# Memory rows turned in two column parts, two first products that trade banks, and later transfers in segment 0

## The chip, the cores and the metric

The kernel runs on one core of a Trainium2 chip. A core has TensorE (PE, matrix products; its weight loads are shown apart as PEld), VectorE (DVE), ScalarE (ACT), GpSimd (POOL) and SyncE (SP, which here only issues DMAs). Each works through its own instructions in order; semaphores hold an instruction until others have finished. SBUF is the working memory of 128 partitions, PSUM the memory that matrix products write to, in eight banks of 512 fp32 columns. The metric is device microseconds of one execution; the time of a kernel is the median of its runs.

## The reference, cut to what matters

The program is two blocks on x of 2048 rows by 640. The first is attention that runs through the rows in 64 segments of 32 rows, with 8 memory rows that each segment hands to the next:

```python
for s in range(n_seg):                      # 64, one after the other
    xs = x[:, s*seg_len:(s+1)*seg_len, :]   # 32 rows, normalised before
    h = concatenate([mem, xs], axis=1)      # 40 rows
    q, k, v = h @ Wq, h @ Wk, h @ Wv        # 32 heads of 128, from 640
    scores = where(mask, q @ k.T * scale, -1e9)
    o = softmax(scores) @ v @ Wo            # 40 rows of 640
    mem = o[:, :8]                          # the next segment's memory
    outs.append(o[:, 8:])
h  = x + concatenate(outs)
h2 = h + (relu(layernorm(h) @ w1 + b1) ** 2) @ w2 + b2
```

The memory makes the segments a chain: no query, key or value of a segment can be finished before the output rows of the memory of the segment before it.

## The kernel before, in words

The order of the instructions on every engine is the order of the program (a manual schedule), written out by hand; buffers come from pools, and a buffer is free again when the last reader in that order has been passed.

One segment is one call of `step`. Its 32 "main" columns are the 8 memory rows and the first 24 rows of the segment; they lie transposed in hT (640 in five chunks of 128, chunk c at column c x 160). The last 8 rows of each segment (the "tails") do not depend on the memory in their projections, so four segments' tails are projected together, as spare units of four matmuls that a planner (`plan`, `portion`) spreads over the segments at about eight a segment. The lists fill, late, mid and nook hold spare units, turns of evacuated tails, and statistics and normalisations of coming blocks; `run` and `run_late` take from them at fixed places.

On TensorE a segment runs: first query product (16 of the 32 heads, 20 matmuls, four to each chunk), first key product, second query product, second key product, memory scores (sm), value products, token scores, some spare units, values (po), the output product of the memory columns (pw, 64 matmuls, line 268), spare units, the token values of the segment before, spare units. Then the next segment's first query product needs the memory.

The way from pw to it: `wo_out` has ScalarE copy two halves of the partitions of pw crosswise into tmp (lines 281 and 282, name otmp), VectorE adds them to the blocks of pw on its own partitions (line 283) and gives o, 128 partitions by 160 columns, five groups of 32. `mem_to_hT` has VectorE turn o in 32 x 32 squares into hT (line 374): group f of o gives the memory columns of chunk f.

PSUM: the pool mm has three banks that rotate (`mmtile`), chn has one (tag ch, used in turn by pw, the first query product pq, and sm twice), pop has four (po; `potile` borrows them for px). In the last segment `end_output` puts the output product of an earlier segment, in chn, between the second query product and the first key product, which in this segment comes only there.

SP issues nearly all DMAs, in order. At the start it loads Wv, Wq, Wk and Wo. Tail values go to a DRAM buffer vt_d, row by row (line 337), and come back in another order as vt (line 394). Some rows wait in buffers that are needed later ("parked"); their stores stand in the list writes. Before the first segments the loop runs up to four of these stores, and in segment 0 loads x of block 1 and the tail values of segments 1 to 3. Then segment 0 runs its spare units (`SEG0`, in four portions among its output product), whose rows are stored when they are ready; their four row buffers are the ones that segment 1's query and key rows take next.

## Time and profile before

| | us |
|---|---|
| median of 3 runs (lowest to highest) | 974.47 (972.43 to 975.36) |
| the profiled execution, its own time | 971.71 |
| its span | 969.6 |
| PE busy | 937.7 (97%) |
| PEld busy | 546.9 (56%) |
| DVE busy | 652.6 (67%) |
| ACT busy | 524.5 (54%) |
| POOL busy | 280.5 (29%) |

The granted TensorE clock is 0.998 of full speed over the span. A line of the timeline gives start, duration, engine, line of the kernel, operation, what it writes and reads, the shape, and how many such instructions are merged; in brackets is idle time of the engine before it and what ended it. "PE pq L232" is a product into the tile pq; L232 is the helper `proj`, so all projections have this line. A matmul's end is modelled, and its duration overlaps the next, so lengths of work on PE are read from starts. In the list of waits each row has microseconds in total, number of times, and the longest.

### The profile page before, as it was taken

The page shows a single profiled execution, that of the slowest core. Times are in us where ns is not written, and L with a number is a line of the kernel's source. Part 1 is how long each engine was busy: PE and PEld are TensorE (multiplying, and loading weights), DVE is VectorE, ACT ScalarE, POOL GpSimd, SP SyncE. Part 2 cuts the span into 40 slices and gives each one's busy share as a digit, 9 for nine tenths or more (in the row PEclk, how much of TensorE's full clock was granted, in tenths as well). Part 3 has the DMA queues.
Part 4 walks back from the last instruction along what each step waited for, and adds up shares of the span by engine and source line. Part 5 has one row for each costly group of instructions (what it writes and reads, how often), then busy time and mean ns, then how long its engine had stood idle before and what let it go on. Part 6 is the DMA issues. An engine that isn't in the chain of part 4 may idle for free.

```text
span 969.6 us, 55554 instructions
## 1 busy us (share of the span) xinstructions
PE 937.7 (97%) x24749; PEld 546.9 (56%) x24760; DVE 652.6 (67%) x1942; ACT 524.5 (54%) x1271; POOL 280.5 (29%) x870
## 2 busy tenths in 40 slices
PE   6978999999999999999999999999999999999998
PEld 2445555555555555555555656555555656555555
DVE  5256777677777767777767676777776777566542
ACT  2445656565566655656656565656555655523321
POOL 2122323233223232322232323232323233253300
PEclk9999999999999999999999999999999999999999
DMA  9981100010010101010102010101010211543320
GB/s 357 399 275 45 23 17 20 19 27 21 19 27 18 30 14 31 9 32 7 37 9 32 13 31 12 33 12 33 12 33 6 53 40 23 182 125 80 98 55 28
DMA packets 65871, 56.62 MB, mean 58 GB/s; under 512 B 37384, under 2 KB 61712, under 8 KB 63712
## 3 DMA queue, kind: packets, MB, share of 16 engines
q1 hardware_dynamic: 65392, 52.74, 19.0%
q8 instruction: 194, 3.18, 1.4%
q14 instruction: 45, 0.37, 0.1%
q0 software_dynamic: 224, 0.33, 0.1%
q10 hardware_dynamic: 16, 0.01, 0.0%
HBM read 38.37 MB, written 9.44 MB: 49 GB/s over the span
## 4 chain that ended last, share of the span: by engine, by line
PE 85%; DVE 5%; DMA 4%; SPq 2%; ACT 2%; issue 1%; POOL 0%; ACTq 0%; DVEq 0%; POOLq 0%
PE ps L232 27%; PE pw L268 15%; PE px L232 13%; PE pq L232 7%; PE y L1012 6%; PE ps L960 6%; PE ps L268 3%; PE po L522 2%; DMA wq<-in_A_Wq_dram 2%; PE po L415 2%; SPq L149 2%; PE sm L486 1%; PE ps L575 1%; DMA wo<-in_A_Wo_dram 1%; DVE kT L476 1%
## 5 line engine op out<-in xcount | busy, mean ns | idle before, releaser
L232 PEld LDWEIGHTS <-hT 128*32 128x32 bf16 x7680 | 192.2, 96 | 191.5 <-DVE hT L374 23.4
L268 PE MATMUL pw<-wo,oT 128*32 128x320 bf16 x4224 | 160.9, 300 | 3.5 <-issue 1.8
L232 PE MATMUL ps<-wk,hT 128*32 128x512 bf16 x2520 | 158.0, 379 | 0.0
L268 PEld LDWEIGHTS <-oT 128*32 128x32 bf16 x4224 | 120.3, 97 | 40.6 <-DVE oT L242 19.4
L256 DVE STREAM_TRANSPOSE qT<-row 128x512 bf16<-128x512 bf16 x128 | 90.7, 709 | 62.4 <-ACT row L251 59.3
L639 POOL TENSOR_TENSOR pkt<-ek,rk 128x64 bf16<-128x64 bf16 x64 | 18.8, 294 | 274.3 <-DVE rk L637 274.3
L232 PE MATMUL ps<-wv,hT 128*32 128x512 bf16 x1260 | 89.6, 378 | 0.0
L232 PE MATMUL pq<-wq,hT 128*32 128x512 bf16 x1260 | 79.8, 381 | 8.6 <-DVE hT L374 6.2
L244 ACT CAST row<-ps 128x512 bf16<-128x512 f32 x105 | 61.8, 591 | 38.1 <-PE ps L232 37.9
L426 ACT CAST oT<-po 128x512 bf16<-128x512 f32 x128 | 68.7, 589 | 20.1 <-PE po L420 19.3
L232 PE MATMUL px<-wq,hT 128*32 128x512 bf16 x1260 | 79.1, 379 | 0.0
L232 PE MATMUL px<-wv,hT 128*32 128x512 bf16 x1260 | 79.0, 378 | 0.0
L434 POOL COPY qz<-qT 128x96 bf16<-128x96 bf16 x126 | 33.4, 265 | 155.7 <-DVE qT L256 155.6
L968 ACT ACTIVATE wv<-ps,b1f 128x512 bf16<-128x512 f32 (+1 forms) x56 | 37.6, 672 | 66.7 <-PE ps L960 66.3
L633 ACT ACTIVATE ek<-tk 128x320 bf16<-128x320 f32 x64 | 30.1, 471 | 72.6 <-DVE tk L628 63.9
L232 PEld LDWEIGHTS <-hTt 128*32 128x32 bf16 x1920 | 46.8, 97 | 29.4 <-issue 5.0
L256 DVE STREAM_TRANSPOSE kT<-row 128x512 bf16<-128x512 bf16 x65 | 46.1, 709 | 21.5 <-ACT row L244 21.5
L1012 PE MATMUL y<-wq,wk 128*128 128x320 bf16 x416 | 58.9, 299 | 0.2
L473 ACT CAST row<-ps 128x256 bf16<-128x256 f32 x126 | 40.7, 375 | 27.7 <-PE ps L232 27.7
L251 ACT ACTIVATE row<-px 128x512 bf16<-128x512 f32 x63 | 37.6, 597 | 30.6 <-PE px L232 30.6
L486 PEld LDWEIGHTS <-qz 128*32 128x32 bf16 x2016 | 34.9, 94 | 33.2 <-POOL qz L436 3.4
L251 ACT ACTIVATE row<-pq 128x512 bf16<-128x512 f32 x63 | 37.6, 597 | 28.7 <-PE pq L232 23.8
(129 smaller groups left out, 1671.6 us busy)
## 6 DMA issues: line engine op xcount, KB each, us to landing
wv<-in_A_Wv_dram SPq DMA_DIRECT2D x5, 1024.0 KB
wq<-in_A_Wq_dram SPq DMA_DIRECT2D x5, 1024.0 KB
wk<-in_A_Wk_dram SPq DMA_DIRECT2D x5, 1024.0 KB
wo<-in_A_Wo_dram SPq DMA_DIRECT2D x8, 640.0 KB
o_all<-o SPq DMA_DIRECT2D x256, 7.5 KB
vt<-vt_d SPq DMA_DIRECT2D x60, 64.0 KB
xt<-in_A_x_dram SPq DMA_DIRECT2D x19, 160.0 KB
wq<-in_B_w_dram SPq DMA_DIRECT2D x1, 2080.0 KB
```

Source lines behind the costliest of these rows:

```text
L232: nc.tensor.matmul(ps[32 * k:32 * k + 32, :], lhsT=lhs(c), rhs=wr[:, c, n, k], start=(c == 0), stop=(c == DC - 1))
L244: nc.scalar.copy(out=out_, in_=in_)
L251: nc.scalar.mul(out=row, in_=ps, mul=scale)
L256: nc.vector.transpose(out=dst[:, n * 16:(n + 1) * 16, 0:32], in_=row.rearrange("p (h e) -> p h e", e=32))
L268: nc.tensor.matmul(pw[32 * j:32 * j + 32, c0:c0 + DH], lhsT=lhs(p), rhs=wov2[:, head(p), ch], start=(h == 0), stop=(h == 15))
L426: nc.scalar.copy(out=oTg[:, gs, :, 0:SEG], in_=po[1][h][:, :, 0:256].rearrange("p g (i q) -> p g i q", q=32))
L434: nc.gpsimd.tensor_copy(out=d.rearrange("p a (j f) -> p a j f", j=3)[:, :, :, 0:M], in_=src[:, :, 0:3, :])
L473: nc.scalar.copy(out=row[:, u * 256:(u + 1) * 256], in_=ps[:, u * 256:(u + 1) * 256])
L486: nc.tensor.matmul(sm[32 * g:32 * g + 32, 0:NK], lhsT=qz[:, p, :], rhs=kT[:, p, :], start=(j == 0), stop=(j == 3), skip_group_check=True)
L960: nc.tensor.matmul(ps[:], lhsT=w1[:, c, fc * 128:(fc + 1) * 128], rhs=hnT[:, c, :], start=(c == 0), stop=(c == DC - 1))
L968: nc.scalar.activation(out=r[:, 0:w], in_=ps[:, 0:w], func=ACT.Relu, bias=b1f[:, fc:fc + 1], scale=1.0)
L1012: nc.tensor.matmul(y[hh][:, 0:DH], lhsT=f1T[:, fc, k * 128:(k + 1) * 128], rhs=w2[:, fc, cs], start=(fc == 0 and not hf), stop=(fc == FFUL ...
```

## The change

`wo_out` gets an argument `then`. With it (all segments but the last, which makes no memory), copies, add and turn run for columns 0 to 95 (chunks 0 to 2) first and then for 96 to 159 (chunks 3 and 4); without it (the tails and the last outputs) nothing changes. The first query product takes a bank of mm in place of chn's, the first key product chn's in place of one of mm. The fourth portion of spare units in segment 0 is called with 5 in place of 9. The load of x for block 1, the load of the tail values of segments 1 to 3 and the parked stores no longer run ahead of segment 0 but ahead of segment 1, that is, behind the row stores of segment 0; the parked stores come after the two loads. Statistics and normalisation of block 1 move one segment on.

```diff
-    def wo_out(pw):
+    def wo_out(pw, then=None):
...
-        nc.scalar.copy(out=five(tmp[0:64]), in_=blocks(64, 128, 0))
-        nc.scalar.copy(out=five(tmp[64:128]), in_=blocks(0, 64, 64))
-        nc.vector.tensor_tensor(out=five(o[:]), in0=blocks(0, 128, 32), in1=five(tmp[:]), op=ALU.add)
+        for c0, c1 in ((0, 3), (3, DC)) if then else ((0, DC),):
+            cs = slice(c0, c1)
+            nc.scalar.copy(out=five(tmp[0:64])[:, cs], in_=blocks(64, 128, 0)[:, cs])
+            nc.scalar.copy(out=five(tmp[64:128])[:, cs], in_=blocks(0, 64, 64)[:, cs])
+            nc.vector.tensor_tensor(out=five(o[:])[:, cs], in0=blocks(0, 128, 32)[:, cs], in1=five(tmp[:])[:, cs], op=ALU.add)
+            if then:
+                mem_to_hT(o, *then, cs)
         return o
...
-    def mem_to_hT(o, b, sp):
+    def mem_to_hT(o, b, sp, cs=slice(0, DC)):
...
-        nc.vector.transpose(out=hc[:, :, at:at + SEG], in_=o[:].rearrange("p (c f) -> p c f", f=32))
+        nc.vector.transpose(out=hc[:, cs, at:at + SEG], in_=o[:].rearrange("p (c f) -> p c f", f=32)[:, cs])
...
-            if which == "q":
-                ps = potile(1) if n else chn.tile([128, 512], F32, tag="ch", name="pq")[:]
+            if which + str(n) == "q1":
+                ps = potile(1)
+            elif which + str(n) == "k0":
+                ps = chn.tile([128, 512], F32, tag="ch", name="pk0")[:]
             else:
                 ps = mmtile()
...
-            o = wo_out(pw)
-            mem_to_hT(o, (s + 1) // 4, (s + 1) % 4)
+            o = wo_out(pw, ((s + 1) // 4, (s + 1) % 4))
...
-    SEG0 = (0, 1, 8, 9)
+    SEG0 = (0, 1, 8, 5)
...
             run(soon, 1)
-            if b == 0:
+            if b == 0 and sp == 1:
+                tails_v_in(0, nc.sync, 1, 4)
+                load_x(1)
+            if b == 0 and sp:
                 run(writes, 4)
-            if b == 0 and sp == 0:
-                load_x(1)
-                tails_v_in(0, nc.sync, 1, 4)
-            if b == 0 and sp == 1:
-                late.insert(0, (1.15, lambda: ln_stats(1), 1))
+            if b == 0 and sp == 2:
+                late.insert(0, (1.15, lambda: ln_stats(1), 2))
                 mid.append(lambda: ln_norm(1))
```

## The prediction

> **What bounds the kernel now.** I read the page's engine shares first, then the list of waits, then the timeline of single segments, last the end of the attention part.

> ```profile
> PE 937.7 (97%) x24749; PEld 546.9 (56%) x24760; DVE 652.6 (67%) x1942; ACT 524.5 (54%) x1271; POOL 280.5 (29%) x870
> ```

> TensorE is the bound: 937.7 us busy of 969.6, so all its idle time is about 32 us, the kernel's start included. An edit on other engines wins only where TensorE waits. From the list of waits (us in total, times, longest):

> ```profile
> ACT otmp L281 <- PE pw L268: 41.7, 65, 1.6
> DVE o L283 <- ACT otmp L282: 41.0, 71, 6.6
> PEld L232 <- DVE hT L374: 23.4, 55, 1.9
> ACT row L251 <- DMA vt_d<-row: 4.6, 1, 4.6
> PE pq L232 <- DVE hT L374: 6.2, 7, 1.5
> ```

> Weight loads wait for the turned memory rows (hT) before 55 segments, matmuls before only 7. The timeline says why: first segment 2, which has no spare work behind its output product, then segment 43, which has.

> ```profile
> 77.41 0.29 ACT L281 COPY otmp<-pw 64x160 f32<-64x160 f32 x1 [0.51 <-PE pw L268]
> 77.71 0.28 ACT L282 COPY otmp<-pw 64x160 f32<-64x160 f32 x1
> 78.02 0.32 DVE L283 TENSOR_TENSOR o<-pw,otmp 128x160 bf16<-128x160 f32 x1 [0.37 <-ACT otmp L282]
> 78.38 0.34 DVE L374 STREAM_TRANSPOSE hT<-o 128x160 bf16<-128x160 bf16 x1
> 78.78 1.26 PE L232 MATMUL pq<-wq,hT 128*32 128x512 bf16 x20 [1.03 <-DVE hT L374]
> 79.87 1.25 PE L232 MATMUL ps<-wk,hT 128*32 128x512 bf16 x20
> ```

> ```profile
> 581.19 0.83 PE L232 MATMUL ps<-wv,hTt 128*32 128x512 bf16 x12
> 581.46 0.34 DVE L374 STREAM_TRANSPOSE hT<-o 128x160 bf16<-128x160 bf16 x1
> 581.86 1.26 PE L232 MATMUL pq<-wq,hT 128*32 128x512 bf16 x20
> ```

> From the first copy to the first query matmul the chain takes 78.78 - 77.41 = 1.37 us everywhere. A product of 20 matmuls advances by 79.87 - 78.78 = 1.085 us, 0.217 for each of its five column chunks. In segment 43 twelve spare matmuls (0.65 us) from 581.19 fill TensorE to 581.84: the chain ends just in time and nothing is lost. Going through all 63 segments by the starts of the matmuls, idle time beyond the usual spacing stands before eleven: 1 (1.5 us), 2, 3, 15, 63 (1.0 to 1.1), 11, 56, 61 (0.7 to 0.8), 7, 60 (0.4), 52 (0.2). Two have 0.1 and about nine 0.06. Some 9 us in all, which is what a shorter chain can touch.

> **Splitting the memory rows (columns 0 to 95, then 96 to 159).** Four instructions become eight in each of 63 segments: two more ACT copies, one more add, one more transpose. Durations by width, interpolated: ACT copies take 288 and 283 ns at 160 columns, and a cast out of PSUM 265 at 128 and 375 at 256, so 0.85 ns a column: 235 and 208 ns for 96 and 64. The add: 324 at 160, TENSOR_TENSOR 491 at 320, 1.04 a column: 257 and 224. The transpose: 345 at 160, 202 to 245 at 64: about 265 and 225. Gaps: copy to copy 12 ns, ACT to DVE 32, add to transpose 34, DVE to weight load 54, DVE to ACT 94 (tk to ek, L628 to L633).

> Part one, from the first copy: copies end at 0.48, the add at 0.77, the transpose at 1.065; the query product starts at 1.12 instead of 1.37, 0.25 earlier. Its first three chunks last 0.65, so it needs part two at 1.77.

> Part two depends on whether ScalarE may read the bank pw while VectorE adds out of it. The nearest row, two copies out of disjoint columns of one bank:

> ```profile
> 30.32 1.04 ACT L244 COPY hTt<-pt 128x384 bf16<-128x384 bf16 x1 [0.65 <-PE pt L208]
> 31.39 0.74 DVE L242 COPY hTt<-pt 128x256 bf16<-128x256 bf16 x1 [6.35 <-ACT hTt L244]
> ```

> VectorE needed only what TensorE had done, yet starts 31 ns after ScalarE's end, three times of three. So I let the second pair of copies wait for the first add: 0.77 + 0.094 = 0.86, copies to 1.28, add 1.315 to 1.54, transpose to 1.80, weights at 1.85. The query product then stands 0.08 before its fourth chunk and ends 0.17 earlier than before; with the bank shared freely part two is there at 1.64 and the gain is 0.25. [...]

> So 11 x 0.17 = 1.9, plus 0.2 and 9 x 0.06 = 0.5: **-2.6 us**. Covered segments gain nothing and should lose nothing: their product starts at about 1.31 to 1.37 of the chain, needs part two at 1.96 or later, and has it at 1.85. Behind it on ScalarE wait the casts of po (L426), which start up to 0.7 later where they followed at once and 0.4 later in segment 43 (0.93 after the first copy, now 1.30). They end by 2.4; the second query product, which takes their bank, starts at 3.5. On VectorE everything behind the first transpose is 0.5 later; the flips of the next queries have 0.3 us of idle time ahead of them, those of the second half 1.0, in all but segments 59 and 61 (0.2 and 0.5), where sums and statistics for the dense part crowd VectorE: +0.1 each, **+0.2**. SP's stores of o wait for the second add, 0.6 later; nothing queued behind them is due within a segment.

> **Banks.** The first query product now takes a rotating bank, in the place of the first key product, so as many are taken per segment, in the same order. Each was last used by scores, values or spare tiles evacuated before pw ended: no wait, 0. The key product in pw's bank starts 1.08 after the query product, when the second add is long done (1.54 against 2.28): 0, and the scores find its evacuation (584.31 to 584.89 in segment 43) done by 586.19: 0. But in the last segment an output product of an earlier segment stands between them:

> ```profile
> 830.81 2.35 PE L268 MATMUL pw<-wo,oT 128*32 128x320 bf16 x64
> 832.98 2.33 PE L232 MATMUL ps<-wk,hT 128*32 128x512 bf16 x40
> 833.20 0.29 ACT L281 COPY otmp<-pw 64x160 f32<-64x160 f32 x1 [1.52 <-PE pw L268]
> 833.82 0.32 DVE L283 TENSOR_TENSOR o<-pw,otmp 128x160 bf16<-128x160 f32 x1 [1.39 <-ACT otmp L282]
> ```

> The key product now needs that bank and must wait for the add: 833.82 + 0.32 + 0.05 = 834.2 instead of 832.98. All of the key, value and dense work is queued behind it on TensorE: **+1.2 us**, at least 0.9 if the dense weights' 0.3 us wait goes.

> **The later transfers.** In segment 1 ScalarE waits for a store:

> ```profile
> 66.45 2.64 SPq L337 DMA_DIRECT2D vt_d<-row  x4
> 69.05 0.60 ACT L251 ACTIVATE row<-pq 128x512 bf16<-128x512 f32 x1 [4.57 <-DMA vt_d<-row]
> 71.04 0.28 PE L486 MATMUL sm<-kT,qz 128*32 128x40 bf16 x16 [1.26 <-DVE kT L256]
> ```

> SP issues four parked stores (60.40), the load of x (62.97) and four loads of tail values (63.58 to 66.35) before segment 0's four row stores. Put behind, the row stores go out from 60.4 as their rows are ready (the last at 63.87) and land some 2.5 us after issue, the first by 63 and the last by 66.5; the casts need them at 66.4 and 69.5. The scores then follow 4.33 after the query product, as in segment 2 (78.78 to 83.11): 69.61 instead of 71.04, 1.43, of which 0.13 returns because segment 1 now runs 3.96 from scores to output product against 4.09 in segment 2: **-1.3 us** (0 to 1.43). The tail values are issued from 64.4 to 67.0, land about 69.5 and are needed at 72.2. The statistics of block 1 move to segment 2, where VectorE has 2.0 us idle before the second query flip and takes 1.1 + 0.5. The count 9 turned 5 changes nothing: ten spare units of four matmuls are left there (40 matmuls from 55.90 to 62.81), and 0 + 1 + 8 leave one.

> **Sum.** -2.6 + 0.2 + 1.2 - 1.3 = -2.5 us. The profiled execution took 971.71 (span 969.6), so 969.2; it stands 2.8 under the median of the runs, 974.47, which gives **972.0**.

> **Rivals.** (1) Slower: part two comes late in every segment. It has 1.96 - 1.85 = 0.11 us to spare where spare work covers the chain. If no piece costs less than the next rows up (265 for each copy, 292 for each add as VectorE's cast in L242, 345 and 245 for the transposes), the first query matmul moves only to 1.30, the last weights come at 2.16 and each of 62 segments loses about 0.14: 8.7 us in place of the 2.6 won, 983. It decides from 0.11 us more than I computed. For it: the covers end just in time, and a copy cut in two pays a fixed share again, here 235 + 208 - 288 = 0.155 us; against: every row shrinks with its width. [...] (2) The bank is shared freely: 0.25 in eleven segments, 3.5 with the small ones, 971.1. (3) The last segment's wait vanishes in the dense part's own waits: 970.8; against it, TensorE runs without a gap from 832.98 on. (4) The tail values come late in segment 1 and take back what the row stores gave: 973.3; against it, 2.7 us to spare.

> **How the numbers follow.** What a measurement here can tell from no change is about 0.3%, 2.9 us. Forecast 0.57; its own range is 970.5 to 974.1 (stores 1.43 and 0.9 at the end, and a scatter of the runs of about a microsecond; on the other side half of the split and 1.1 for the stores): 0.24 of it beyond 2.9, 0.33 within. Rival 1: 0.20, of it 0.16 slower, 0.04 within. Rival 2: 0.11, 0.08 faster. Rival 3: 0.08, 0.07 faster. Rival 4: 0.04, 0.01 slower. Together faster 0.39, same 0.44, slower 0.17. The range 969.0 to 977.0 leaves out the far part of rival 1 and the meeting of rivals 2 and 3.

> **What would show it.** Right: otmp copies at about 235 and 208 ns; the third copy some 94 ns after the first add; in segment 2 the query product 0.25 earlier, with a wait of under 0.1 inside; no wait for a store in segment 1; a new wait of 1.2 us before the last key product. Wrong: a wait for the second transpose in most segments, covers that no longer meet the chain, or a new wait of segment 1's values for their load.

## The result

The kernel after takes 971.07 us (median of 12 runs, 969.55 to 974.71) where the kernel before takes 973.34 beside it (12 runs, 972.03 to 976.16). The ratio is 0.9972, 95% interval [0.9961, 0.9983]: 0.28% or 2.7 us faster, by a hair less than the 0.3% that the prediction called the limit of what can be told. The profiled execution took 970.47 us (span 968.5) against 971.71 (span 969.6). A second measurement of the same order of instructions, in the last experiment below, gives 0.9965 [0.9954, 0.9977].

### The profile page after: what moved, and what is told of

It reads as the page before. It is cut to its first block, busy times and chain, and to the rows that moved or that the text cites. A ratio compares the mean times of both kernels' runs of the same rounds, so it can differ in the third digit from the quotient of the medians.

```text
span 968.5 us, 55767 instructions
## 1 busy us (share of the span) xinstructions
PE 938.5 (97%) x24749; PEld 552.2 (57%) x24760; DVE 670.0 (69%) x2068; ACT 541.1 (56%) x1397; POOL 282.2 (29%) x870
## 4 chain that ended last, share of the span: by engine, by line
PE 90%; DVE 6%; ACT 2%; issue 1%; DMA 0%; POOL 0%; ACTq 0%; DVEq 0%
PE ps L232 30%; PE pw L268 16%; PE px L232 12%; PE pk L232 7%; PE y L1017 6%; PE ps L965 6%; PE ps L268 4%; PE po L528 2%; PE po L419 2%; PE sm L492 1%; PE pa L232 1%; DVE kT L482 1%; PE ps L581 1%; DVE pmem L514 1%; ACT em L501 1%
## 5 line engine op out<-in xcount | busy, mean ns | idle before, releaser
L232 PEld LDWEIGHTS <-hT 128*32 128x32 bf16 x7680 | 197.7, 96 | 184.0 <-DVE hT L378 15.4
L268 PE MATMUL pw<-wo,oT 128*32 128x320 bf16 x4224 | 162.2, 300 | 4.1 <-issue 2.3
L268 PEld LDWEIGHTS <-oT 128*32 128x32 bf16 x4224 | 119.9, 97 | 42.7 <-DVE oT L242 18.9
L256 DVE STREAM_TRANSPOSE qT<-row 128x512 bf16<-128x512 bf16 x128 | 89.6, 700 | 43.3 <-ACT row L251 43.0
L232 PE MATMUL ps<-wv,hT 128*32 128x512 bf16 x1260 | 89.7, 378 | 0.0
L232 PE MATMUL ps<-wq,hT 128*32 128x512 bf16 x1260 | 80.0, 380 | 6.1 <-DVE hT L378 5.9
L232 PE MATMUL pk<-wk,hT 128*32 128x512 bf16 x1260 | 79.3, 379 | 1.1 <-DVE o L285 1.1
L232 PE MATMUL ps<-wk,hT 128*32 128x512 bf16 x1260 | 79.3, 379 | 0.0
L232 PE MATMUL px<-wq,hT 128*32 128x512 bf16 x1260 | 79.3, 379 | 0.0
L232 PE MATMUL px<-wv,hT 128*32 128x512 bf16 x1260 | 79.1, 378 | 0.0
L283 ACT COPY otmp<-pw 64x96 f32<-64x96 f32 (+2 forms) x129 | 28.9, 224 | 64.7 <-PE pw L268 44.0
L232 PEld LDWEIGHTS <-hTt 128*32 128x32 bf16 x1920 | 47.2, 97 | 29.8 <-issue 5.3
L285 DVE TENSOR_TENSOR o<-pw,otmp 128x96 bf16<-128x96 f32 (+2 forms) x129 | 31.4, 243 | 43.7 <-ACT otmp L284 41.7
L251 ACT ACTIVATE row<-ps 128x512 bf16<-128x512 f32 x93 | 54.3, 606 | 9.9 <-PE ps L232 7.9
L256 DVE STREAM_TRANSPOSE kT<-row 128x512 bf16<-128x512 bf16 x65 | 46.0, 707 | 16.8 <-ACT row L244 16.5
```

The lines of the kernel that those rows point to most:

```text
L232: nc.tensor.matmul(ps[32 * k:32 * k + 32, :], lhsT=lhs(c), rhs=wr[:, c, n, k], start=(c == 0), stop=(c == DC - 1))
L251: nc.scalar.mul(out=row, in_=ps, mul=scale)
L256: nc.vector.transpose(out=dst[:, n * 16:(n + 1) * 16, 0:32], in_=row.rearrange("p (h e) -> p h e", e=32))
L268: nc.tensor.matmul(pw[32 * j:32 * j + 32, c0:c0 + DH], lhsT=lhs(p), rhs=wov2[:, head(p), ch], start=(h == 0), stop=(h == 15))
L285: nc.vector.tensor_tensor(out=five(o[:])[:, cs], in0=blocks(0, 128, 32)[:, cs], in1=five(tmp[:])[:, cs], op=ALU.add)
```

## The profile after

First the engine shares, from the page of the kernel after. TensorE is as busy as before; VectorE and ScalarE have 126 instructions more, two for each of 63 segments, and some 17 us more to do.

```profile
PE 938.5 (97%) x24749; PEld 552.2 (57%) x24760; DVE 670.0 (69%) x2068; ACT 541.1 (56%) x1397; POOL 282.2 (29%) x870
```

Second the list of waits of the kernel after (us in total, times, longest). The weight loads' wait for hT (line 378) has shrunk from 23.4 us before 55 segments to 15.4 before 41. The third line is new: in 63 segments ScalarE's second pair of copies waits 0.33 us for VectorE's first add. The wait of `row` for the store into vt_d is gone from the list.

```profile
ACT otmp L283 <- PE pw L268: 44.0, 65, 1.9
DVE o L285 <- ACT otmp L284: 48.0, 134, 6.6
ACT otmp L283 <- DVE o L285: 20.6, 63, 0.4
PEld L232 <- DVE hT L378: 15.4, 41, 1.6
PE ps L232 <- DVE hT L378: 5.9, 8, 1.3
```

Third the timeline of segment 2, with nothing to cover the chain (start, duration, engine, line, what is written and read, the shape; in brackets the idle time before it and what ended it).

```profile
76.48 0.24 ACT L283 COPY otmp<-pw 64x96 f32<-64x96 f32 x1 [0.51 <-PE pw L268]
76.73 0.23 ACT L284 COPY otmp<-pw 64x96 f32<-64x96 f32 x1
76.99 0.26 DVE L285 TENSOR_TENSOR o<-pw,otmp 128x96 bf16<-128x96 f32 x1 [0.27 <-ACT otmp L284]
77.28 0.21 ACT L283 COPY otmp<-pw 64x64 f32<-64x64 f32 x1 [0.33 <-DVE o L285]
77.28 0.28 DVE L378 STREAM_TRANSPOSE hT<-o 128x96 bf16<-128x96 bf16 x1
77.51 0.20 ACT L284 COPY otmp<-pw 64x64 f32<-64x64 f32 x1
77.62 1.30 PE L232 MATMUL ps<-wq,hT 128*32 128x512 bf16 x20 [0.79 <-DVE hT L378]
77.74 0.23 DVE L285 TENSOR_TENSOR o<-pw,otmp 128x64 bf16<-128x64 f32 x1 [0.18 <-ACT otmp L284]
78.00 0.24 DVE L378 STREAM_TRANSPOSE hT<-o 128x64 bf16<-128x64 bf16 x1
78.30 1.42 PEld L232 LDWEIGHTS <-hT 128*32 128x32 bf16 x32 [0.35 <-DVE hT L378]
78.74 1.25 PE L232 MATMUL pk<-wk,hT 128*32 128x512 bf16 x20
```

From the first copy to the first query matmul it is now 77.62 - 76.48 = 1.14 us instead of 1.37. The fourth chunk's weights are loaded at 78.30, 1.82 after the first copy. Inside the product the largest step between two matmuls is 0.23 against 0.22 before, and the memory scores follow the product's start by 4.36 against 4.33: 0.24 won and 0.04 given back, 0.20 net.

Fourth the boundary of segments 0 and 1 in the timeline after. The four row stores go out from 60.38, the tail values behind them; the cast of the query rows waits for no store, and the scores come 4.36 after the product's start (65.68) where it was 5.76 (65.28 to 71.04).

```profile
60.38 4.52 SPq L341 DMA_DIRECT2D vt_d<-row  x4
65.00 2.77 SPq L398 DMA_DIRECT2D vt<-vt_d  x4
67.08 0.60 ACT L251 ACTIVATE row<-ps 128x512 bf16<-128x512 f32 x1 [1.31 <-issue]
70.04 0.27 PE L492 MATMUL sm<-kT,qz 128*32 128x40 bf16 x16
```

Last the last segment of the kernel after. The key product waits for the add that reads its bank: it starts 831.73 - 830.34 = 1.39 us after the last matmul of the output product, where before it followed in 0.13.

```profile
830.74 0.29 ACT L283 COPY otmp<-pw 64x160 f32<-64x160 f32 x1 [1.57 <-PE pw L268]
831.36 0.32 DVE L285 TENSOR_TENSOR o<-pw,otmp 128x160 bf16<-128x160 f32 x1 [1.45 <-ACT otmp L284]
831.73 1.26 PE L232 MATMUL pk<-wk,hT 128*32 128x512 bf16 x20 [1.10 <-DVE o L285]
```

So each of the three moves shows at its place. What each is worth in the time, a single pair of traces does not tell: TensorE has stalls of 0.45 to 0.8 us that no wait explains (between 66 and 830 us seven in the trace before, eight in the one after), at other places in each trace, and the sections below find a larger one. The experiments undo the parts one at a time.

## The experiments

All ratios are to the kernel before, run on the same chip beside them.

**The parts undone, one at a time.** First the split: copies, add and turn undivided again, all else as after.

```diff
-        for c0, c1 in ((0, 3), (3, DC)) if then else ((0, DC),):
+        for c0, c1 in ((0, DC),):
```

> The changed kernel with copies, add and turn of the memory rows undivided again; banks and transfers as changed. Theory (the split is worth about 0.2 us in each of eleven held segments and 0.06 in about nine more): slower than the changed kernel by 2.5 to 3.0 us, that is within 0.05% of the kernel before, and in segment 2 the query product again 1.37 us after the first copy instead of 1.14. Rival (the gain comes from transfers and banks alone): equal to the changed kernel, 0.28% under the one before.

Measured: 972.74 us (970.38 to 974.18), ratio 0.9995 [0.9984, 1.0005]. In the timeline of its segment 2 the first query matmul is back at 76.69 - 75.32 = 1.37 after the first copy:

```profile
75.32 0.29 ACT L283 COPY otmp<-pw 64x160 f32<-64x160 f32 x1 [0.51 <-PE pw L268]
...
76.69 1.26 PE L232 MATMUL ps<-wq,hT 128*32 128x512 bf16 x20 [1.04 <-DVE hT L378]
```

The split is worth 0.9995 - 0.9972 = 0.23%, 2.2 us, uncertain by some 1.5 (2.9 against the second measurement of after's order, 0.9965). Added up segment by segment from this trace to the one after, the way from the first copy to the product is 4.1 shorter and the way from the product to the scores 0.2 longer: twelve segments without cover give 0.24 - 0.04 each, twelve whose cover ended just in time 0.04 to 0.12, the covered ones 0.01. Transfers and banks alone, the rival here, leave the time where it was before.

Next the order of the transfers: the load of x, the tail values, the parked stores and the statistics of block 1 back at their old places, the split kept. They go back together, so this doesn't tell which of them counts.

```diff
-            if b == 0 and sp == 1:
-                tails_v_in(0, nc.sync, 1, 4)
-                load_x(1)
-            if b == 0 and sp:
+            if b == 0:
                 run(writes, 4)
-            if b == 0 and sp == 2:
-                late.insert(0, (1.15, lambda: ln_stats(1), 2))
+            if b == 0 and sp == 0:
+                load_x(1)
+                tails_v_in(0, nc.sync, 1, 4)
+            if b == 0 and sp == 1:
+                late.insert(0, (1.15, lambda: ln_stats(1), 1))
```

> The changed kernel with the loads, parked stores and the statistics of block 1 back where they were before; split and banks as changed. Theory: the cast of segment 1's first queries waits for the row store again (about 4.5 us on ScalarE), the scores of segment 1 come 5.7 to 5.8 us after its query product instead of 4.36, and the kernel is 1.3 us slower than the changed one, about 0.14% under the one before. Rival (the transfers are hidden either way): equal to the changed kernel.

Measured: 973.45 us (969.47 to 974.91), ratio 0.9996 [0.9984, 1.0008]: 0.24% or 2.3 us slower than after, uncertain by some 1.6; the forecast was 1.3. In its timeline the row stores go out at 67.41, a microsecond later than in the kernel before; the scores start 72.01 - 64.29 = 7.72 after the query product, not 5.76.

```profile
67.41 1.99 SPq L341 DMA_DIRECT2D vt_d<-row  x4
70.02 0.60 ACT L251 ACTIVATE row<-ps 128x512 bf16<-128x512 f32 x1 [5.64 <-DMA vt_d<-row]
72.01 0.33 PE L492 MATMUL sm<-kT,qz 128*32 128x40 bf16 x16 [3.18 <-DVE kT L256]
```

In this execution the wait costs more than its length. Windows of the same trace (length, then the busy time of PE, PEld, DVE, ACT and POOL with the number of instructions, then the granted TensorE clock, DMA share and GB/s):

```profile
68.00:70.00 2.00, 0.82 (x16) 0.21 (x8) 0.00 (x0) 0.00 (x0) 0.47 (x1) 1.00 0.77 226
70.00:72.00 2.00, 0.00 (x0) 0.10 (x1) 1.35 (x3) 1.98 (x5) 0.52 (x3) 0.86 0.91 262
72.00:74.00 2.00, 1.99 (x36) 0.98 (x39) 1.66 (x7) 0.52 (x3) 0.93 (x4) 0.50 0.61 162
74.00:76.00 2.00, 2.00 (x76) 1.13 (x64) 0.59 (x5) 1.05 (x4) 0.00 (x0) 0.79 0.29 97
```

TensorE idles for some 3 us, and then the granted clock is 0.50 from about 71.4 to 74.8, so the scores and values behind the wait run at half speed. By windows of 1 us, the clock that is missing here adds up to 1.71 us. The traces of before and of after lose the same 1.7 us, but in segment 0, where this one loses nothing (last section). Over the twelve runs it comes out nearly even: by their granted clocks, those of this kernel had 1.0 such stretches on average (none in three runs, one in six, two in three), those of after 0.8 (none in two, one in ten). So the half clock makes little of the 2.3 us; most of it is the wait itself.

Third the wait in the last segment: only there, the first key product in a rotating bank again.

```diff
-            elif which + str(n) == "k0":
+            elif which + str(n) == "k0" and not last:
```

> The changed kernel, but in the last segment the first key product takes a rotating bank, as before the change. Theory: the wait of 1.10 us before the last key product goes, nothing takes its place, and the kernel is 1.2 us faster than the changed one, about 0.40% under the one before. Rival (the dense part waits for its own weights, so the stall is absorbed): equal to the changed kernel, a wait for weights of about 1 us at the first dense product.

Measured: 969.23 us (965.48 to 970.26, 6 runs), ratio 0.9953 [0.9935, 0.9971], 0.19% or 1.8 us under after, uncertain by some 2, so that the time alone shows only that it is faster than before. In the timeline the key product follows at once, but the first dense product then waits for its weights:

```profile
830.49 2.35 PE L232 MATMUL ps<-wk,hT 128*32 128x512 bf16 x40
836.20 2.33 PE L965 MATMUL ps<-hnT,wq 128*128 128x512 bf16 x9 [0.51 <-DMA wq<-in_B_w_dram]
```

From the same start of the last segment's query product (826.00 and 825.96) the key product comes 1.24 earlier than after, the first dense product 836.86 - 836.20 = 0.66. That weights' wait isn't bound to the edit: in the run with fewer spares below, which has the edit too, it is absent.

Fourth the other way round, the banks traded in the kernel before and nothing else.

```diff
-            if which == "q":
-                ps = potile(1) if n else chn.tile([128, 512], F32, tag="ch", name="pq")[:]
+            if which + str(n) == "q1":
+                ps = potile(1)
+            elif which + str(n) == "k0":
+                ps = chn.tile([128, 512], F32, tag="ch", name="pk0")[:]
```

> The kernel before with the two first products' banks traded, and nothing else. Theory: no segment's first query product waits for a rotating bank (start 1.37 to 1.38 after the first copy as before, scores 4.33 after it), and in the last segment the key product starts 1.40 after the output product ahead of it instead of 0.13: 1.27 us there, of which the dense part's wait for weights gives back about half: 0.6 to 1.2 us slower than before, ratio 1.0006 to 1.0012. Rival (the trade is what won, or it costs in every segment): a ratio below 0.999 or above 1.003.

Measured: 974.01 us (972.45 to 975.09) beside 972.23, ratio 1.0017 [1.0008, 1.0026], 1.7 us slower. Where the chain decides, the query product starts 1.37 to 1.38 after the first copy and the scores come 4.33 behind it, as before; so no rotating bank is late. The list of waits of this kernel has one new line, the last segment's:

```profile
PE pk L232 <- DVE o L283: 1.0, 1, 1.0
```

So the trade costs only in the last segment, by the trace 1.22 us of later key product (1.35 instead of 0.13 after the output product), of which 1.15 is left at the first dense product: the dense part gave back 0.07 and not the half that was expected. The time says 0.8 to 2.5.

Put together: 0.23% for the split, 0.24% for the transfers, 0.17 to 0.19% against them for the bank. That is 0.28 to 0.30%, what the whole change measured; each part is uncertain by 0.1 to 0.2%.

**How much room part two has.** Its turn is issued twice, which makes it one transpose later.

```diff
             if then:
                 mem_to_hT(o, *then, cs)
+                if c0:
+                    mem_to_hT(o, *then, cs)
```

> The changed kernel with the turn of part two made twice, so that part two is ready about 0.27 us later; nothing else. Theory (part two has some 0.15 us to spare where spare work covers the chain, none elsewhere): 0.12 us lost in each of about 49 covered segments and 0.27 in each held one, 9 us in all, 0.6 to 0.8% slower than the one before, with a wait for the second turn inside the query products. Rival (part two is hidden in the first three chunks with room to spare): equal to the changed kernel.

Measured: 977.42 us (976.20 to 978.64), ratio 1.0045 [1.0031, 1.0058], 0.73% or 7.1 us slower than after, and 0.45% slower than before, where 0.6 to 0.8% was expected. In the segments without cover the step of the query product to its fourth chunk is now 0.51 and the scores come 0.28 later; in most covered ones 0.08 to 0.10; where the cover ends just in time 0.12 to 0.20; in the seven whose cover lasts longer nothing. The sum over the trace is 7.6 us. A transpose of 0.24 with its gap is 0.27, so covered segments had 0.18 to spare in the kernel after.

**Where to cut.** At 64 columns instead of 96:

```diff
-        for c0, c1 in ((0, 3), (3, DC)) if then else ((0, DC),):
+        for c0, c1 in ((0, 2), (2, DC)) if then else ((0, DC),):
```

> The kernel after, cut at 64 columns instead of 96. From the widths measured after (0.24 and 0.23 for copies of 96 columns, 0.21 and 0.20 of 64, add 0.26 and 0.23, turn 0.28 and 0.24): part one has copies to 0.42, add to 0.69, turn to 0.96, so the first query product starts about 1.02 after the first copy instead of 1.14. Part two: copies from 0.73 to 1.21, add to 1.51, turn to 1.83, weights at 1.88. But the product now needs part two after two chunks of 0.217, at 1.45, and stands 0.43. Theory (the product's start and the last chunk's arrival both count): memory scores then come 4.33 + 0.4 after the product's start, which makes held segments end about 0.2 us later than after (2.4 us over twelve) and covered ones, which start at 1.36 and need part two at 1.79, lose about 0.09 each (some 4 us over fifty): 5 to 7 us slower than after, ratio about 1.003 to 1.005. Rival (what counts is the start, the product's wait is hidden in its pipelining): 0.12 us won in each held segment, 1.4 us faster than after, ratio 0.9960.

Measured: 974.53 us (973.24 to 977.49) beside 972.23, ratio 1.0027 [1.0016, 1.0037], 0.55% or 5.3 us slower than after, at the low end of the forecast. In the timeline of its segment 2 the product starts 77.25 - 76.23 = 1.02 after the first copy, eight matmuls run, and the twelve others wait:

```profile
76.23 0.21 ACT L283 COPY otmp<-pw 64x64 f32<-64x64 f32 x1 [0.51 <-PE pw L268]
77.25 0.61 PE L232 MATMUL ps<-wq,hT 128*32 128x512 bf16 x8 [0.67 <-DVE hT L378]
...
78.09 0.83 PE L232 MATMUL ps<-wq,hT 128*32 128x512 bf16 x12 [0.22 <-DVE hT L378]
```

The step there is 0.60, the scores come 0.37 later, for 0.12 of earlier start; most covered segments lose 0.05 to 0.23. Summed over the segments, 7.4 lost and 1.2 won. The theory holds: the start alone is not what counts.

At 128 columns:

```diff
-        for c0, c1 in ((0, 3), (3, DC)) if then else ((0, DC),):
+        for c0, c1 in ((0, 4), (4, DC)) if then else ((0, DC),):
```

> The kernel after, cut at 128 columns. Part one has about 0.26 and 0.25 for the copies, 0.29 for the add and 0.32 for the turn: first query product about 1.24 after the first copy. Part two of 32 columns: copies about 0.18 each from 0.85 to 1.24, add 0.2, turn 0.2, weights at about 1.8, while the product needs them after four chunks, at 1.24 + 0.87 = 2.1. Theory: nothing stands inside the product (step 0.22, scores 4.33 after it), held segments win 0.14 in place of 0.21 and just-in-time ones still 0.06: 0.8 us slower than after, ratio 0.998 by that kernel's 0.9972; covered segments lose nothing. Rival (two cuts of about the same worth, or the shorter second part wins): level with after or faster.

Measured: 969.10 us (966.51 to 971.56) beside 972.87, ratio 0.9963 [0.9950, 0.9976]. In its trace the product starts 1.26 after the first copy and has no step inside (0.22, scores 4.33 behind): each of the twelve segments without cover loses 0.08 against after, 1.0 in all, and the others nothing, near what was expected. The time doesn't bear that out: 0.998 was expected, which lies outside the interval, and the ratio is level with the kernel after (0.9965 beside it, in the last experiment), as the rival has it. So between 96 and 128 columns only the trace decides, and for 96.

**What the second copies wait for.** They write the tile otmp that the first add reads, and read the bank that it reads. This kernel gives the second part another buffer.

```diff
             cs = slice(c0, c1)
+            if c0:
+                tmp = s2.tile([128, DQ], F32, tag="otmp", name="otmp")
```

> The kernel after, where the second part's copies go to another buffer than the first part's. Theory (it is the bank pw, which the add reads, that holds the second copies): the third copy still starts 33 ns after the first add's end and waits for it in 63 segments; time as after, ratio 0.9972. Rival (it is the buffer tmp): the third copy starts right behind the second, 0.3 earlier, part two's weights are there 0.2 earlier, the step before the fourth chunk goes back from 0.23 to 0.22 and nothing stands inside the product; about 0.03 us in each of twelve segments, 0.4 us in all, so the time hardly tells but the list of waits does.

Measured: 968.45 us (967.07 to 969.78), ratio 0.9957 [0.9944, 0.9970]. Its list of waits has the same line as after's:

```profile
ACT otmp L285 <- DVE o L287: 20.6, 63, 0.4
```

So another buffer doesn't free the second copies; what they still share with the first add is the bank pw, and behind it they stand in all 63 segments, 20.6 us in all, though both only read it. The prediction took that order from three pairs of copies, where VectorE's began 31 ns after ScalarE's end. The uncovered segments run as in the kernel after (1.14, 0.23 and 4.36), and the rival's 0.4 us would not explain the lower ratio either; its interval overlaps that of after, 0.9972, and more that of the second measurement, 0.9965. What else lies in it stays open. A kernel that lets ScalarE read the bank beside the add wasn't tried.

**Fewer spare units inside segment 0's output product.** Five units of four matmuls left there move behind it, where TensorE waits 1.59 us for segment 1's memory rows; with the last segment's key product as in the third experiment.

```diff
-    SEG0 = (0, 1, 8, 5)
+    SEG0 = (0, 1, 4, 0)
```

> The kernel after with the last segment's key product back in a rotating bank (as in the run on the last key) and the third and fourth counts of spare units in segment 0 at 4 and 0 in place of 8 and 5: five units of four matmuls (1.09 us) move from inside segment 0's output product to behind it, where TensorE waits 1.6 us for segment 1's memory rows. Theory: that wait shrinks by 1.1 and the output product ends 1.1 earlier, 1.1 us faster than the run on the last key (0.9953): ratio about 0.994. Rival (segment 0 is held there by something else, the instructions' supply or the weights Wo): the output product starts no earlier, or the wait moves ahead of it, and the ratio stays at 0.995.

Measured: 966.90 us (964.72 to 967.29, 5 runs) beside 972.23, ratio 0.9941 [0.9927, 0.9955], the fastest of all. Its timeline shows 18 spare matmuls between the output product and the query product, which now starts 0.47 after the last of them, where the step was 1.59:

```profile
61.85 0.32 PE L268 MATMUL pw<-wo,oT 128*32 128x320 bf16 x2
61.99 1.26 PE L232 MATMUL ps<-wv,hTt 128*32 128x512 bf16 x18
63.34 1.30 PE L232 MATMUL ps<-wq,hT 128*32 128x512 bf16 x20
67.70 0.27 PE L492 MATMUL sm<-kT,qz 128*32 128x40 bf16 x16
```

The query product starts 2.40 earlier than in the third experiment, of which 1.12 is this wait; the rest belongs to the clock, below. In the time the difference from the third experiment is 0.12% or 1.2 us, the 1.1 that was forecast, with an uncertainty of 2.2.

The same counts in the kernel before, alone:

```diff
-    SEG0 = (0, 1, 8, 9)
+    SEG0 = (0, 1, 4, 0)
```

> The kernel before with the third and fourth counts of spare units in segment 0 at 4 and 0 in place of 8 and 9, and nothing else. In the kernel with later transfers this edit brought segment 1's query product 2.4 us forward. Theory (in the kernel before, segment 1's scores start by the row stores behind SP's other transfers and not by TensorE): the query product comes at about 62.8 in place of 65.28, the four row stores still go out from 66.4 to 68, the cast that waits for them still starts at 69.0 and the scores at 71.0; the wait grows from 4.6 to about 7 us and the time stays as before, ratio 0.9995 to 1.0005. Rival (the start of the scores follows TensorE): scores 2 us earlier, ratio about 0.998.

Measured: 973.91 us (971.36 to 976.59) beside 972.87, ratio 1.0008 [0.9996, 1.0021]: nothing won. The query product comes 1.70 earlier (63.58; the trace of before had lost 1.7 us of clock ahead of it, this one had not), but the scores 0.65 later than in the kernel before (71.69 for 71.04), since the row stores go out at 67.06. And behind the wait TensorE runs at half clock, for twice as long as in the run with the old transfers (3.41 us of clock lost against 1.71); from its windows:

```profile
70.00:72.00 2.00, 0.32 (x20) 0.37 (x24) 1.67 (x3) 1.82 (x5) 0.72 (x3) 0.63 0.89 255
72.00:74.00 2.00, 2.00 (x27) 0.82 (x20) 1.34 (x7) 0.39 (x2) 0.72 (x3) 0.50 0.51 122
74.00:76.00 2.00, 2.00 (x40) 0.95 (x36) 0.88 (x6) 0.97 (x3) 0.00 (x0) 0.50 0.47 144
```

Segment 2's query product is at 81.60, 2.82 later than before. So with the old order of the transfers, segment 1's scores start by SP's queue, and an earlier TensorE only waits longer; with the new one they follow TensorE. The theory has that right and, as in the run with the old transfers, misses the clock. Here it shows in the runs too: seven of the twelve have a granted clock of 0.996, two such stretches, against five of the 69 runs of the kernel before.

**The count of segment 0, nine or five.**

```diff
-    SEG0 = (0, 1, 8, 5)
+    SEG0 = (0, 1, 8, 9)
```

> The kernel after with the fourth count of segment 0 at 9 again. The prediction has it that only one unit is left there, so that 9 and 5 are the same. Theory: the timeline of segment 0 is that of after (forty spare matmuls in the output product), and the ratio lies in after's interval, 0.9961 to 0.9983; it shows besides how far two measurements of one order of instructions lie apart. Rival (the count matters): four units more or less in the output product, 0.9 us.

Measured: 969.14 us (968.14 to 970.26, 9 runs) beside 972.87, ratio 0.9965 [0.9954, 0.9977], a ratio inside after's interval. The two kernels have the same instructions in the same order on every engine, so the count does nothing, as predicted, and the two ratios show how far two measurements of one order can lie apart: 0.07%. One thing differs between the two traces, and it is not the program. Windows of segment 0 in the kernel after, then in this one:

```profile
58.00:60.00 2.00, 1.27 (x20) 1.16 (x23) 0.39 (x2) 0.00 (x0) 1.23 (x3) 0.70 1.11 349
60.00:62.00 2.00, 2.00 (x26) 0.99 (x22) 0.00 (x0) 0.00 (x0) 0.00 (x0) 0.50 0.91 267
```

```profile
58.00:60.00 2.00, 0.52 (x16) 0.48 (x19) 0.69 (x3) 0.47 (x1) 0.58 (x2) 1.00 1.10 345
60.00:62.00 2.00, 2.00 (x49) 1.27 (x44) 0.00 (x0) 0.59 (x1) 0.65 (x2) 1.00 0.96 284
```

## Why the prediction was right, and where not

The forecast was 972.0, that is 2.5 us under before, as a sum of -2.6 + 0.2 + 1.2 - 1.3. The change is worth 2.7 by the ratio; the 0.9 between 972.0 and 971.07 is mostly the kernel before, which took 973.34 beside it and not the 974.47 that the forecast started from. The sum came out nearly right, but its terms partly by luck: by the times of the experiments the stores won 1.0 more than forecast, the split 0.2 less, and the bank cost 0.5 more, which leaves 0.3.

- **Split, -2.6.** The mechanism is as forecast: 1.14 from the first copy (forecast 1.12), the second copies behind the first add in all 63 segments, part two's weights at 1.82 (forecast 1.85). The net gain in a segment without cover is 0.20, not 0.17. The mis-sized piece is the handover from VectorE to ScalarE: the copy starts 34 to 36 ns after the add's end, 63 times, while the forecast took 94 ns from a subtraction and the exponential behind it. With twelve such segments, one more than counted (segment 24), and 1.4 us in the others, where 0.7 was forecast, the trace's sum is 3.9, the time's 2.2 with an uncertainty of 1.5; the forecast lies between, and why the time shows less than the trace stays open. The widths were priced well: copies of 0.24, 0.23, 0.21 and 0.20, adds of 0.26 and 0.23, turns of 0.28 and 0.24, against 0.235, 0.208, 0.257, 0.224, 0.265 and 0.225 in the forecast. Cut in two the copies take longer in sum (four 0.88, where two took 0.57), but that is paid beside other work.
- **Covered segments lose nothing.** Right. The spare is 0.18 (0.11 forecast, and 0.06 of the difference is again 94 against 35 ns). The first rival, 983 us from 0.11 late, was the right thing to fear: 0.27 late costs 7.1 us, and a cut at 64 columns 5.3.
- **VectorE crowded in segments 59 and 61, +0.2.** 59 gives 0.14 (4.32 to 4.46 from product to scores); 61 only the 0.04 of every uncovered segment. So 0.14 in place of 0.2.
- **Banks 0, last segment +1.2.** Right: 1.27 between the traces, 1.22 in the run with the banks alone, and 0.17 to 0.19% in the time. The third rival, that the dense weights' wait absorbs it, happened in part in one trace (0.51 of it) and not in another.
- **Row stores, -1.3, at most 1.43.** This is the term that was wrong. The wait before segment 1's scores was read as a fixed 1.43. It is the difference between two times that move apart: the stores' landing (in the four kernels with the old order, before, banks alone, before with fewer spares, and old transfers, the waiting cast starts at 69.05, 69.45, 69.70 and 70.02) and TensorE's arrival (query product at 65.28, 64.73, 63.58 and 64.29). Beyond the usual 4.33 to 4.36 from product to scores the wait took 1.43, 2.38, 3.78 and 3.36. In the kernel before's own trace TensorE was late, because segment 0 had run at half clock (1.71 us lost), so the wait looked short; with the banks alone segment 0 ran at full clock (nothing lost). Undone, the order costs 2.3 us, uncertain by 1.6. The upper bound of the range of this term should have been the wait that follows when segment 0 ends early, not the wait of the one trace.
- **Count 9 to 5: nothing.** Right.

By the times (2.3 against 1.3 for the stores, 2.2 against 2.6 - 0.2 for the split, 1.7 against 1.2 for the bank) each of these differences is within the uncertainty of a difference of two ratios, so the times alone don't show that the stores' term failed; the waits of the four traces do. The second rival, a bank read by both freely, is refuted by the 63 waits; the fourth, late tail values, by the absence of any wait for vt in segment 1 of after.

## What to carry to other kernels

Cut a chain's handover in two only where the first part feeds the consumer long enough: the second part must be there before the consumer has used up the first, here 0.65 us of matmuls for 0.68 of handover; a cut one chunk earlier turned a gain into a loss. Price a wait that ends with a DMA from both sides, by when the transfer lands and by when the engine arrives, since one trace shows only one difference of the two. And when a bank is reassigned, look at the one place where the usual order of its users is different, here the last segment: that exception ate over a third of the gain. Taking it out gave 0.9953, and with five spare units moved into the next hole 0.9941.

## What the runs showed of the hardware

**A clock at half speed.** In segment 0 TensorE stands still for 2.2 to 2.5 us (an "issue" stall from 56 or 57 us on, in all traces; 2.40 between two starts in before, 2.34 in after). Behind it the clock is 0.50 in seven of thirteen traces and 1.00 in six, with the same instructions in after (half) and in the run with count nine (full). Each time the loss is the same, 1.69 to 1.71 us summed over windows of 1 us, so 3.4 us at half speed (in before from 57.92 to 61.33, in after from 58.78 to 62.20); the run of the kernel before with fewer spares loses 3.41, twice that, behind its longer wait.

It reaches the time where nothing hides it. Of the runs of after, the two with a granted clock of 1.0 took 969.55 and 969.87, the ten with 0.998 (one such stretch) 971.37 in the median. Over the 77 runs of the nine kernels with the new order of the transfers a stretch goes with 1.5 us more (0.9 to 2.2, a line fitted within each kernel), over the 69 runs of the kernel before with 0.2 (-0.4 to 0.8); there, as its trace shows, a late TensorE shortens the wait for the stores. So this event is a part of the scatter of single runs, and not all of it. Of the 2.40 us by which the query product comes earlier in the fastest kernel than in the third experiment, some 1.3 are then not the edit's: that experiment's trace is one of the seven.

**The stall itself.** The list of waits names no cause. The DMA records point to one: blocks of instructions (queue q8, 194 packets of 16 KB for TensorE's 49,500 instructions) come 255 of its instructions apart in the mean (in after from 56 to 435, the 435 at 838 us without such a stall), but here 409 to 424 after the block before (413 in before, 421 in after), and the last matmul ahead of the stall starts 0.02 to 0.22 us after that packet, in all thirteen traces (0.21 in before, 0.04 in after). So TensorE may well be waiting for its own instructions; no run changes that, and it stays open.

**A handover.** VectorE to ScalarE took 34 to 36 ns where ScalarE copies out of the bank that VectorE had read, and mostly 93 to 95 ns (43 of 64 segments in the traces of before and of after, 115 or 116 in 19) where it computes an exponential of what VectorE wrote.
